# Long-short attention and a softplus FFN on one core: the same tasks issued in another sequence

## The chip, the cores and the metric

The program runs on one core of a Trainium2 chip. The core has five engines that work side by side, each through its own queue of instructions, strictly in order: TensorE (PE, matrix products; its weight loads appear apart as PEld), VectorE (DVE), ScalarE (ACT), GpSimd (POOL), and SyncE (SP), which here issues all transfers between device memory and on-chip memory. The metric is device time in microseconds for one execution.

## The reference

The inputs are q, k, v (4 batches, 8 heads, 768 positions, 64 wide) and two weight matrices. Every query looks at the keys less than 16 positions away and at 24 block summaries: of each block of 32 positions the elementwise maximum of the keys and the mean of the values. The result goes through a feed-forward network (FFN) with softplus between two products.

```python
k_sum = k.reshape(B, H, nb, block, D).max(axis=3)
v_sum = v.reshape(B, H, nb, block, D).mean(axis=3)
scores_l = scale * np.matmul(q, k.transpose(0, 1, 3, 2))
mask_l = np.abs(pos[:, None] - pos[None, :]) < window
scores_s = scale * np.einsum('bhsd,bhnd->bhsn', q, k_sum) + np.log(block)
scores_all = np.concatenate([np.where(mask_l, scores_l, -1e9), scores_s], axis=-1)
a = softmax(scores_all)
attn = np.matmul(a, np.concatenate([v, v_sum], axis=2))
h = x @ w_in            # x: 3072 tokens x 512, w_in: 512 x 2048
g = np.maximum(h, 0.0) + np.log1p(np.exp(-np.abs(h)))
return g @ w_out        # w_out: 2048 x 512
```

## The kernel before

**Tiling.** The 3072 tokens are six groups of 512. A group is two chunks of 256 queries, and each chunk is done for two head pairs at a time (hp 0 and 2). One such attention step is: scores on PE (line 653), mask and row maximum on DVE (666), exponent and row sum on ACT (674), inverse of the sum on DVE (681, 682), normalization on POOL, DVE or ACT (687, or eight instructions at 690), a transposition (for the first group on PE, for later ones on DVE at 720, and then out to device memory and back, 727 and 732), the product with the values on PE (751), and a copy of the result (763).

**The FFN.** The 2048 hidden columns are 16 blocks f. For float32 accuracy every operand is kept as a high part and a remainder, and a product takes three matmuls. The first product of groups 0 and 1 over blocks 0 to 7 is plain (line 1055); elsewhere a pair of blocks and two halves of the tokens are multiplied with seven products in place of eight (1095), which DVE combines from PSUM (the additions of line 1105, and a copy at 1114 or 1115). Softplus is two ACT instructions (1157, 1161) and a remainder on DVE (1165). The second product (1172) accumulates in PSUM.

**Operands.** Splitting a weight tile is a chain through one scratch tile t: magnitude (929 on DVE, 932 on ACT), clamp (936), shift (940), sign (944), tail (950 on ACT, 953 on DVE), addition of the tail on POOL (958), high part (962), remainder (969). Sums of weights for the seven-product form are joined (995), combined (1003 to 1006), rounded (1019) and given a remainder (1026) in a scratch tile ws. The sums of v of a batch are made in a scratch tile st (393 to 398), the maxima of k read a scratch tile kf. The attention's results are prepared in the same manner (differences at 821 and 822, high part at 806, remainder at 813). The tiles t, ws, st, kf and the output tile ob share one ring of two buffers, so a tile is only given out when the one two before it is done.

**The phases.** Blocks 0 to 7 for groups 0 to 4, then all 16 blocks for group 5, then blocks 8 to 15 for groups 4 down to 0. Attention of a group runs beside the FFN of the group before. The first half of the weights is split early in the kernel, the second half beside group 5's FFN. Below, f5.10 is block 10 of group 5.

**What sets the order.** All work is first recorded as 2346 numbered tasks with their reads, writes and buffers; a task may have several ways, each on another engine. Then a table written out in the source, SEQUENCE, gives the task numbers in the order in which they are issued; a letter behind a number picks another way than the first ("a" the second, "b" the third). Each engine gets its instructions in the order of this table. Waits come from the data and buffers alone.

```python
for word in sequence.split():
    task = self.tasks[int(word.rstrip("abc"))]
    assert all(other in begun for other, _ in task.after) and task not in begun
    begun.add(task)
    task.ways[" abc".index(word[-1]) if word[-1] in "abc" else 0].run()
```

Of the kernel before, what the change touches and what calls it, by code (L numbers as in the profile page):

```python
# [147 lines left out]
0 4 5 6 7 8 9 10 11 12 13 14 15 16 17 18 19 20 21 150 22 23 24 25 26 48 44 45 49 46 54 55 60 151 3 47 52 94 27 66 28  # L148
29 30 31 160 67 152a 50 156a 153 32 100 33 34 80 35 68 169 36 37 38 39 2 40 41 311 1 154 155 42 43 312 101 81 157 56
314 69 51 161a 53 106 61 162 165a 158 163 62 70 313 164 310 178 107 71 73 82 159 102 120 83 170 72 166 171 174 172 173  # L150
121 319 74 108 109 57 96 84 63 322 175 167 176a 58 177 168a 95 110 183a 64 103 65 323 122 370 123 59 187 97 179a 180
341 181 182 324 344 371 75 104 98 343 342 184 185 325 85 186a 340 99 105 374 326a 78 76 327 86 196 79 87 88 89 77 197
111 188a 189 113 90 92 134 349a 91 112 190 93 352 387 191 388 389 114 135 138 124 192 115 193 125 127 375 118 116 117
126 353 128 198 194 390 206 328 315 316 129 119 141 130 202 199 200 132 396a 354 391 201 244 133 215 195a 131 207 355
321 208 317 203 147 209 211 204 329 318 253 245 216 205 399 210 246 254 356 247 372 248 332 249 357 400 250 251 260
252 320 255 234 261 256 212 213 262 263 330 257 137 331 139a 214 144a 333 225 221 376 136 258 373 217 218 259 219 220
377a 264 334 358 417 418 265 345 346 401 419 267 421 222 266 268 223a 380 224 359 402 362 235 230 226 338a 145 420 227
228 361 146 148 274 229 350 403b 351 269 347 404 360 348 140 275 270 336a 381 378 271 231 276 277 405 278 232a 272 233
382 363 379 339a 392 393 236 364 366 368 369 142 237 238 335 281 288 367a 406 282 383 289 426 429 240 283 273 239 430
279 337a 280 290 409 408 407 384 291 531 149 532 284 285 385a 530 143 431 395 394 535a 386 292 295 432 296 538 397 286  # L160
398 297 433a 434 410 298 555 539 241 242 556 243 411 415a 416 435 513a 554 514 422 518 425 519 299 424 287 293 294 413
428 540 423 414 520a 559 303 436 541 437 439 562 302 515 438 300 301 542a 427 543 516 440 441 517a 579 563 578 445 581
582 580 443a 564 544 444 446 533 447 754 587 448 565 536 755 449 590 521a 450 537 758 566 545 451 304 608 611 534 456
457 305 458 567 609 546 548 452 453 610 459 463 464 607 759 465 307a 308a 466 454 547 460 549 591 550a 306 309 568
616a 467 522a 557 561 619 772 773 775 592 455 470 471 558 477 523a 524 756 560 593 478 774 525a 569 570 571 594a 595
461 572 462 472 620 771 473 596 552 766 551 474 757 479 780 573 783 480 762 583 585 481 621 484 485 574a 589 588 486
622 767 623 597 760 763 624 598 487 599 600 584 784 586 764 800 625 488 802 803 576a 468 469 475 476 601 801 785 799
602a 761 612 615 768 613 617 626 553 786 628 604 808a 491 492 493 605 614 765 811 627 498 499 577 618 787 482 788 606
629 603 828 789 575 494 500 812 1051 501 769 495 502 813 770 630 1053 829 631a 635 827 636 633 638 639a 640 641 365
483 642 776 814 634a 643a 777 778 637 644 489 647 645a 815b 832a 650 648 646 655 1052 649 651 653 652 1054 835 656 654  # L170
816 657 658 790 792 782 1055 781 836 659 490 496 412 660 497 503 666 667 853 854 793 837 526 505 852 661 668 527a 528a
857 504 1056 860 671 838 839a 507 672 817 506 529a 674 680 840 662 677 673 510 861 675 678 682 779 683 791 442 996 681
# [24 lines left out]
1351 1352a 1683a 1687a 1344a 1353a 1354 1355 1360 1363 1357 1358 1356 1361 1359 1365 1362 1367 1239 1366 1364 1690a
1369 1368 1370 1240 1376 1377 1371 1378 1237 1236 1372 1456 1241 1242 1457 1458 1459 1818 1461 1474 1243 1381 1460
1382 1387 1384 1385 1383 1386 1388 1392 1389 1390 1462 1391 1393 1394 1475 1476 1479 1463 1373 1374 1396 1375 1379
1395 1477 1397 1401 1478 1402 1398 1403 1406 1408 1814 1492 1464a 1811 1693a 1480 1481a 1482 1493 1407 1409 1412 1380  # L200
1410 1417 1415 1808 1411 1494 1413 1549 1550 1497 1495 1418 1416 1421 1419 1422 1496 1420 1551 1414 1426 1427 1399
1465 1400 1552a 1423 1428 1498 1499a 1404 1431 1500 1554a 1483 1434 1437 1432a 1435 1553a 1433 1438 1511 1488 1470
1405 1436 1439 1501 1442 1440 1512a 1513 1514 1516 1555 1441 1556 1502 1443 1446 1447 1515 1444 1424 1445 1425 1429
1430 1451 1557 1448 1466 1452 1517 1518 1453 1507 1467 1566 1569 1468 1469 1568 1471 1572 1519 1567a 1570 1472a 1484a
# [1159 lines left out]
```

## Time and profile before

| | |
|---|---|
| three runs | 690.67, 693.21, 697.65 us (median 693.21) |
| the profiled execution | 692.42 us |
| its span, first to last instruction | 690.7 us |
| mean granted TensorE clock | 0.973 |
| busy: PE, PEld, DVE, ACT, POOL | 619.7, 531.2, 489.2, 329.1, 243.2 us |
| moved by DMA | 103.41 MB, mean 150 GB/s |

A view of the trace groups instructions by line, engine, operation and tiles; "x<-r,x 128x512" means that tile x was written from tiles r and x. In groups, the number behind the comma is the mean of one in ns, and what follows the second bar is the idle time before these instructions and who ended it. In a timeline the columns are the start and the duration in us. In the list of waits, "A <- B: total, times, longest" says that A waited for B. The granted clock is the share of full speed that PE was given.

### The profile page before, as it was taken

The numbers are of one execution on the slowest core, as the hardware profiler recorded it, in microseconds if no ns is written. First come the engines' busy times: TensorE is split into PE (matmuls) and PEld (weight loads), VectorE is DVE, ScalarE is ACT, GpSimd is POOL, SyncE is SP. The second block draws the span as 40 slices with busy tenths as digits, with TensorE's granted clock in tenths as the row PEclk, the third lists the DMA queues.
The fourth block names the chain that finished last, engine by engine and source line by source line (L and its number), as shares of the span: only waits on it lengthen the run. The fifth ranks groups of instructions, "written<-read, shape, count | busy, mean of one in ns | idle before, by whom it ended". The sixth has DMA issues, their size and how long they took to land.

```text
span 690.7 us, 13155 instructions
## 1 busy us (share of the span) xinstructions
PE 619.7 (90%) x4880; PEld 531.2 (77%) x4880; DVE 489.2 (71%) x1143; ACT 329.1 (48%) x807; POOL 243.2 (35%) x204
## 2 busy tenths in 40 slices
PE   8876877979989889989989786988999999999997
PEld 8655665767778769878868665777989889899896
DVE  5999878776986676577768898986555655654542
ACT  4785755586686553946615364562331422313220
POOL 4465455425524150131145745463050600502000
PEclk9998999899999999999999998999999999999999
DMA  9888886689997966478345431001313112030031
GB/s 291 184 272 228 244 226 192 196 265 263 240 295 212 228 180 202 149 199 246 125 151 199 151 124 62 0 16 47 123 61 123 33 60 93 1 121 1 21 103 61
DMA packets 86848, 103.41 MB, mean 150 GB/s; under 512 B 27424, under 2 KB 64896, under 8 KB 86016
## 3 DMA queue, kind: packets, MB, share of 16 engines
q1 hardware_dynamic: 86784, 102.58, 50.1%
q8 instruction: 38, 0.62, 0.4%
q14 instruction: 26, 0.21, 0.1%
HBM read 72.88 MB, written 27.26 MB: 145 GB/s over the span
## 4 chain that ended last, share of the span: by engine, by line
PE 54%; DVE 20%; DMA 8%; ACT 6%; SPq 5%; POOL 4%; issue 4%; DVEq 0%; POOLq 0%; ACTq 0%
PE po L1172 24%; PE hx L1095 14%; PE hy L1095 10%; PE xo L751 3%; DMA st<-v_hp_dram 2%; PE sc L653 2%; DVE t L936 2%; DVE sp L666 2%; DMA pT<-squares 1%; DVE w L969 1%; DVE x L813 1%; SPq L732 1%; ACT sp L674 1%; DVE gl L1165 1%; DVE t L944 1%
## 5 line engine op out<-in xcount | busy, mean ns | idle before, releaser
L1172 PE MATMUL po<-w,gh 128*128 128x512 f32 x768 | 207.0, 398 | 0.5 <-ACT gh L1157 0.5
L1172 PEld LDWEIGHTS po<-w,gh 128*128 128x128 f32 x768 | 142.4, 191 | 31.1 <-issue 1.1
L1172 PE MATMUL po<-w,gl 128*128 128x512 f32 x384 | 117.6, 400 | 3.5 <-DVE gl L1165 2.2
L813 POOL TENSOR_TENSOR x<-r,x 128x512 fp32r<-128x512 f32 x36 | 48.3, 1354 | 183.7 <-ACT x L806 100.1
L1157 ACT ACTIVATE gh<-hx 128x512 fp32r<-128x512 f32 x40 | 24.0, 599 | 141.7 <-DVE hx L1105 141.6
L1095 PE MATMUL hx<-x,w 128*128 128x256 f32 x480 | 72.7, 288 | 15.5 <-DVE gl L1165 8.3
L1172 PEld LDWEIGHTS po<-w,gl 128*128 128x128 f32 x384 | 70.7, 190 | 19.8 <-DVE gl L1165 4.6
L1095 PE MATMUL hx<-x,sw 128*128 128x256 f32 x480 | 74.8, 292 | 9.8 <-DVE u L1105 8.0
L1095 PEld LDWEIGHTS hx<-x,w 128*128 128x128 f32 x480 | 65.8, 192 | 22.2 <-DVE gl L1165 10.5
L1095 PEld LDWEIGHTS hx<-x,sw 128*128 128x128 f32 x480 | 64.5, 193 | 13.7 <-DVE u L1105 9.4
L674 ACT ACTIVATE sp<-sp,nm 128x120 f32<-128x120 f32 x192 | 73.0, 382 | 4.1 <-DVE nm L666 3.8
L1095 PE MATMUL hy<-x,sw 128*128 128x256 f32 x480 | 67.9, 285 | 0.7 <-DVE x L813 0.7
L1095 PEld LDWEIGHTS hy<-x,sw 128*128 128x128 f32 x480 | 62.4, 192 | 1.1 <-DVE x L813 0.9
L958 POOL TENSOR_TENSOR t<-t,raw 128x1024 int32<-128x1024 int32 (+1 forms) x20 | 40.3, 2014 | 58.1 <-DVE t L944 33.2
L1055 PE MATMUL ph<-xw,w 128*128 128x512 f32 x192 | 50.2, 410 | 5.1 <-DVE xw L785 4.5
L1055 PEld LDWEIGHTS ph<-xw,w 128*128 128x128 f32 x192 | 36.3, 194 | 15.3 <-DVE xw L785 5.0
L666 DVE CUSTOM_DVE_ANT_0 sp<-sc,added 128x120 f32<-128x120 f32 x192 | 40.7, 277 | 3.4 <-PE sc L653 1.8
L687 POOL TENSOR_TENSOR sp<-sp,ss 128x960 f32<-128x960 f32 x14 | 25.9, 1849 | 48.1 <-ACT x L806 15.5
L1105 DVE TENSOR_TENSOR u<-hy,u 128x256 f32<-128x256 f32 x80 | 30.9, 420 | 14.3 <-PE hy L1095 13.7
L1165 DVE TENSOR_TENSOR gl<-hy,gh 128x512 fp32r<-128x512 f32 x40 | 27.5, 687 | 18.0 <-ACT hy L1161 17.8
L751 PEld LDWEIGHTS xo<-pT,v 120*64 120x64 f32 x640 | 21.0, 140 | 23.6 <-issue 14.9
L751 PE MATMUL xo<-pT,v 120*64 120x64 f32 x640 | 23.6, 227 | 16.3 <-DMA raw<-r 5.3
(115 smaller groups left out, 1036.8 us busy)
## 6 DMA issues: line engine op xcount, KB each, us to landing
squares<-tb SPq DMA_DIRECT2D x20, 512.0 KB
pT<-squares SPq DMA_DIRECT2D x80, 128.0 KB
raw<-w_out_dram SPq DMA_DIRECT2D x16, 512.0 KB
kf<-kT_dram SPq DMA_DIRECT2D x16, 384.0 KB
raw<-w_in_dram SPq DMA_DIRECT2D x6, 1024.0 KB
q<-qT_dram SPq DMA_DIRECT2D x20, 256.0 KB
raw<-r SPq DMA_DIRECT2D x20, 256.0 KB
part<-ob SPq DMA_DIRECT2D x10, 512.0 KB
```

The source lines that it names most:

```text
L666: nc.vector.tensor_tensor_reduce(out=sp()[:, n], in0=unit(n), in1=added()[:, kinds.index((lows[w], lows[w + 1]))], scale=-SCALE, scalar=FL ...
L674: nc.scalar.activation(sp()[:, n], sp()[:, n], AF.Exp, bias=nm()[:, n:n + 1], scale=-1.0, accum_out=ss()[:, n:n + 1],)
L687: engine.tensor_tensor(sp(), sp(), s, op=ALU.mult)
L751: nc.tensor.matmul(xo()[h * D:(h + 1) * D, g * CH + w * QW:g * CH + (w + 1) * QW], lhsT=tiles.v(g)[:, w, h * D:(h + 1) * D], rhs=queries(g ...
L813: engine.tensor_tensor(to(1), a(), to(0).bitcast(F32), op=ALU.subtract)
L958: nc.gpsimd.tensor_tensor(a, a, word(0, I32), op=ALU.add)
L1055: nc.tensor.matmul(ph(), lhsT=lhs(part, cc), rhs=xw[cc][0]()[:, xw[cc][1], a], start=cc == 0 and n == 0, stop=cc == NCC - 1 and n == 2,)
L1095: nc.tensor.matmul(to()[:, half], lhsT=lhs(wa, cc), rhs=of_x(xa)[:, cc * CH:(cc + 1) * CH], start=cc == 0 and m == 0, stop=cc == NG - 1 an ...
L1105: DVE, dve(CH), lambda: nc.vector.tensor_tensor(out(), a(), b(), op=op), reads, [write],
L1157: nc.scalar.activation(gh(), all_of(), AF.Softplus)
L1165: nc.vector.tensor_sub(out=gl(), in0=all_of(), in1=gh().bitcast(F32))
L1172: nc.tensor.matmul(po[t](), lhsT=a()[:, t * P:(t + 1) * P], rhs=w2()[:, part, i2 * DM:(i2 + 1) * DM], start=f == f0 and i == 0, stop=f == ...
```

## The change

Only the table SEQUENCE differs. The tasks, buffers, transfers and their sizes are the same; 151 tasks run on another engine. In all, ACT has 27 tasks more, POOL 16 fewer, DVE 11 fewer. The numbers stay close to their old places (the last quarter is nearly unchanged). Its first lines, and one from the late weight stage:

```diff
-0 4 5 6 7 8 9 10 11 12 13 14 15 16 17 18 19 20 21 150 22 23 24 25 26 48 44 45 49 46 54 55 60 151 3 47 52 94 27 66 28
+160 161a 162 163 0 4 44 46 54 3 5 6 7 8 9 10 11 12 13 14 15 164 165 45 60 151 2 166 47 1 167a 152a 168 55 169 16 17 18
...
-1465 1400 1552a 1423 1428 1498 1499a 1404 1431 1500 1554a 1483 1434 1437 1432a 1435 1553a 1433 1438 1511 1488 1470
+1438 1512a 1405 1436 1516 1555 1439 1442 1443 1513 1446 1444 1556 1424 1425 1445 1514 1515 1451 1447 1429 1452 1517
```

By engine, tasks that move: high parts of attention results from DVE to ACT (17, and 5 back) and their remainders between POOL and DVE (14 to POOL, 12 to DVE), remainders of weights (8) and of weight sums (4) from POOL to DVE, magnitudes (6) and high parts (6, 4 back) of weights from DVE to ACT, normalizations (5 from POOL to DVE, 3 from POOL to ACT), the first copy of a block pair (7 each way between ACT and DVE). The transfers stay on SP, with loads of q, k, v and weights at other places in its queue; the first of all is now a weight tile.

DVE before, late weight stage, from f5.8's two remainders (gl) over the weight sum ws of blocks 12 and 13 to f5.10's first combinations (u):

```order
L1165 TENSOR_TENSOR gl<-hx,gh 128x512
L1165 TENSOR_TENSOR gl<-hy,gh 128x512
L995 TENSOR_TENSOR ws<-w 128x2x2x128 x2
L1003 TENSOR_TENSOR ws<-ws 128x256
L1004 TENSOR_TENSOR ws<-ws 128x256
L1005 TENSOR_TENSOR ws<-ws 128x256
L1006 TENSOR_TENSOR ws<-ws 128x256
L1105 TENSOR_TENSOR u_4914<-hx,p_4900 128x256
L1105 TENSOR_TENSOR u_4922<-hy,u_4914 128x256
```

The same place on DVE now:

```order
L1165 TENSOR_TENSOR gl<-hx,gh 128x512
L1165 TENSOR_TENSOR gl<-hy,gh 128x512
L944 SCALAR_TENSOR_TENSOR t<-raw,t 128x1024
L969 TENSOR_TENSOR w<-t,w 128x512
L995 TENSOR_TENSOR ws<-w 128x2x2x128 x2
L1105 TENSOR_TENSOR u_4930<-hx,p_4905 128x256
L1105 TENSOR_TENSOR u_4932<-hy,u_4930 128x256
```

The four combining instructions of ws have gone to POOL, a remainder of a weight tile (L969) has come from POOL, and a sign (L944) that stood ahead of the gl now stands behind them.

DVE before, some 35 us earlier, from the last combinations of f5.4 to the joined weight sum and f5.6's copy (p):

```order
L1105 TENSOR_TENSOR hy<-u_4578,hy 128x256
L1105 TENSOR_TENSOR hy<-hy,u_4578 128x256
L1019 CAST sw<-ws 128x1024
L1165 TENSOR_TENSOR gl<-hx,gh 128x512
L1165 TENSOR_TENSOR gl<-hy,gh 128x512
L962 CAST w<-t 128x1024
L969 TENSOR_TENSOR w<-t,w 128x1024
L995 TENSOR_TENSOR ws<-w 128x2x2x128 x2
L1115 COPY p_4668<-hx 128x256
```

And now:

```order
L1105 TENSOR_TENSOR hy<-hy,u_4605 128x256
L1105 TENSOR_TENSOR hy<-u_4605,hy 128x256
L1165 TENSOR_TENSOR gl<-hx,gh 128x512
L1165 TENSOR_TENSOR gl<-hy,gh 128x512
L1026 TENSOR_TENSOR sw<-ws,sw 128x1024
L969 TENSOR_TENSOR w<-t,w 128x1024
L995 TENSOR_TENSOR ws<-w 128x2x2x128 x2
```

The rounding of the weight sum (L1019), the high part of a weight tile (L962) and the copy p are on ACT now; the weight sum's remainder (L1026) has come from POOL.

ACT now, at group 1's first blocks, with the third group's attention (sp, scores) between them:

```order
L674 ACTIVATE sp,ss<-sp,nm 128x120 x8
L1157 ACT_TABLE_LOAD
L1157 ACTIVATE gh<-ph 128x512
L1161 ACTIVATE ph<-ph 128x512
L690 ACTIVATE sp<-sp,ss 128x120 x8
L1157 ACTIVATE gh<-ph 128x512
L1206 COPY ob<-po 128x512 x2
L1157 ACTIVATE gh<-ph 128x512
L1161 ACTIVATE ph<-ph 128x512 x2
```

The normalization L690 (eight instructions) was on POOL; it stands between the softplus of one block and that of the next.

More of the change, by code (lines that the diff above doesn't have):

```diff
@@ L153 @@
[L153 to L172, printed above, removed]
@@ new lines @@
+405 382 363 240 285 236 337a 338 420 237 364 366 288 368 238 383 142 406 426 369a 239 289 429 407 430 290 241 409 392
+291 143 140 384 385a 295 386 296 367 531 532 279 530 280 393 535 538 242a 395 394 431 145a 365 432 433b 408 397 243
+292 297 286 513 398 555 298 410 434 556 146 559a 539 554 518a 435 299 422 425 411a 287 293 514 423 428 540 413 519a
+427 415 436 541 520 542a 439 562 294 543 437 515 563 303 516 301 517 302 300 438 416a 424 440 441 578 443 445 446 579
+444 582 521 339a 414a 580 581 544 533 587 564 447 456 448 590 534 565 754 457 536 755 545 449 450 758 546 547 548 608
@@ new lines @@
+451 307a 609 610 611 759 566b 458 537 463 308a 607 464 304 305 567 465 309 459 466 452 453 616a 454 306 591 460 592
+619 467 568 756 772 549 550 455 522a 774 775 557 523a 593 594a 524 560 569 470 471 570 571 472 148 552a 477 478 461
+462 473 595 474 561 620 479 572 558 525a 480 573 481 757 553a 773 551 771 780 596 766 484 485 621 760 783 574 622 468
+623a 469 583 584 589 486 597 475 761 767 588 598 487 585 599 800 600 586 803 576 624 784 476 601 762 802 785 577 801
+488 625 764 763 612 799 786 602a 604 605a 768 787b 626 788 627 491 492 628 808 493 618 629 613 615 498 494 765 769
@@ new lines @@
+665 669 864a 688 691 1007 1024 692 1062 693 865 1008 794 795 1025 1027 818 670 819 696 699 1009 698 1026 804 702 1032a
+805 821 820 697a 700 707 703 701 705 709 706 689 690 708 694 1010 806 704 710 711 810 1023 716 712 807 809 1059 866
+1063 717 713 718 822 823 1035 721 727 722 796 842 830 724 1011 797a 1012 1069 825 834 831 1036 723 844 725 726 728
+1068 845 843 729 732 730 833 734 731 733 736 735 737 741 1070 695 798 714 742 738 743 846 824 1072 847a 1071 715 719
+720 1037 826a 1077 1080 739 849a 1013 850 851a 1060 1064 867 868 1038 855 859 870 856 858 869 1039b 1040 1081 871 740
@@ new lines @@
+848 872 874 1098 1097 876 879 1099 1065 877 882 880 878 881 1100 744 883a 884a 1066 875 885 891 886 894 888 889 887
+1041 895 896 890 745 892 898 897 748a 1101 1082 749a 899 893 1083 1000 1106a 1084 900 901 907 902 1001 908 1006 1014
+1002 1015 1109 1017 1016 909 1003 1005 1085 747 746 903 1018 1110 1245 1246 1019 873 1021 904 912 1067 915 914 918 913
+1249 1244 916 750 751a 921 919 917 923 752a 924 922 925 1042 920 926 927 905 928 1086 929 932 933 906 910 1111 934
+1020 937 1028 1034 1029 1031 940 938a 943 941 948 944 946 949 939 947 942 952 953 911 950 1033 945 951 957 958 954
@@ new lines @@
+1022a 930 1112 1252 1045 1030 753 1044 1043 1113 1268 959 1046 1114 1047 931 1269 962 1253 963 1087 964 965 968 1073
+1088 1272a 966 971 967 973 1267 1090 1078 969 975 972 976 1074 1075 974 1049 935 936 1115 1050 1275 1079 977 978 1076
+970 982 983 1089 1291 1048 979 984 1091 1092a 1094 1116 1254 1095 1299a 1117 1255 1256 1102 955 956 1118 1103 1105
+1104 1257 1119 1108 960 961 980 1107 1120 1276 1096a 1121a 1093 1125 1290 1123 1258 1292 1293 1294 1126 1259 1128 1131
+1127 1261 1129 1130 981 1124 1132a 1133a 1134 1140 985 1135 1143 1137 1247 1251 1277 1260 1144 1136 1138 1145 1139
@@ new lines @@
+1557 1448 1466a 1453 1566 1572 1467 1468 1469 1569 1567a 1570 1518 1568 1501 1571 1471 1430 1811 1573 1577 1519 1472
+1473 1484a 1575 1578 1576 1502 1485 1486 1503a 1579 1581 1574 1504 1530 1580 1487 1489 1505 1582 1583 1586 1587 1588
+1490 1506 1449 1450 1454 1591 1592 1593 1491 1507 1558a 1597 1594 1595 1596 1598 1455 1600 1520 1508 1599 1535 1602
+1509 1601 1603 1559 1604 1606 1605 1607 1611 1612 1510 1608 1584 1613 1560a 1585 1531a 1521 1589 1561 1532 1616 1618
+1617 1625 1533 1619 1534 1522a 1523 1622 1590 1626 1536 1620 1539 1540 1545 1537 1621 1623 1624 1627 1628 1524 1629
@@ new lines @@
+1631 1609 1610 1630 1525 1538 1636 1614 1632 1637 1562a 1526 1615 1527 1563a 1564 1633 1638 1641 1565 1642 1650 1644
+1528 1647 1643 1529 1645 1691 1648 1646 1652 1651 1692a 1634 1653 1687a 1541a 1685 1635 1649 1654 1542 1543 1639 1656
+1544 1655 1657 1694 1640 1658 1661 1662 1663 1546 1686 1695 1688 1809 1689 1812 1942 1948 1696 1699 1702 1697a 1698
+1700 1701 1703 1705 1707 1547 1706 1709 1708 1548a 1659 1711 1704 1710 1810 1660 1712 1718 1713 1719 1815 1720 1664
+1723 1726 1725 1724a 1729 1727 1952 1728 1730 1665 1668a 1734 1732 1733 1736 1735 1669 1666 1738 1813a 1667 1671 1714
```

109 lines of the change are left out of this document (47 added, 62 removed), and 4 rows, old and new, of the table SEQUENCE.

## The prediction

> **What bounds the kernel now.** I read the page's busy shares first, then a table of stages, then the waits inside the two stages that stand out, then single instructions.
>
> ```profile
> PE 619.7 (90%) x4880; PEld 531.2 (77%) x4880; DVE 489.2 (71%) x1143; ACT 329.1 (48%) x807; POOL 243.2 (35%) x204
> 0.00:47.00 47.00, 39.28 (x641) 33.87 (x641) 37.41 (x131) 29.79 (x109) 23.36 (x42) 0.96 0.90 255
> 47.00:127.00 80.00, 61.72 (x451) 46.89 (x450) 69.39 (x152) 45.58 (x115) 46.50 (x37) 0.89 0.78 217
> 127.00:181.00 54.00, 47.94 (x415) 37.60 (x415) 39.32 (x113) 38.26 (x110) 22.14 (x20) 0.97 0.89 257
> 181.00:247.00 66.00, 58.26 (x574) 49.95 (x573) 49.05 (x159) 42.11 (x122) 23.15 (x21) 1.00 0.85 234
> 247.00:355.00 108.00, 103.74 (x952) 88.99 (x951) 75.77 (x210) 61.14 (x170) 22.53 (x16) 1.00 0.60 179
> 355.00:405.00 50.00, 41.23 (x251) 35.16 (x250) 45.01 (x69) 23.97 (x37) 28.50 (x23) 1.00 0.50 175
> 405.00:462.00 57.00, 46.68 (x261) 40.92 (x260) 50.78 (x74) 30.94 (x41) 28.98 (x15) 0.91 0.10 37
> 462.00:477.00 15.00, 10.92 (x63) 10.00 (x62) 12.27 (x16) 3.75 (x6) 9.19 (x6) 0.89 0.16 52
> 477.00:691.00 214.00, 209.96 (x1288) 187.79 (x1286) 110.22 (x224) 53.58 (x101) 38.87 (x29) 1.00 0.20 65
> ```
>
> A stage row gives its length, then busy time of PE, weight load, DVE, ACT and POOL, the granted clock, the DMA share and GB/s. From 247 to 355 and from 477 on, PE is busy for 314 of 322 us at full clock: nothing that only reorders the other engines can help there. PE idles 18 us in 47 to 127 and 23 us (8.8, 10.3, 4.1) in 355 to 477. In both DVE is the busy one (87%, and 108 of 122 us), POOL is at its heaviest (58% and 55%) and the clock is below one. These are the stages in which weights are split into parts. Between them, 127 to 247, DMA is at 85 to 89% and PE loses 14 us. Who ends PE's waits in 350 to 480:
>
> ```profile
> PE hx L1095 <- DVE u L1105: 12.4, 6, 4.3
> PE hx L1095 <- DVE gl L1165: 8.3, 5, 2.9
> ```
>
> So 20.7 us of the late idle time are waits for two kinds of cheap DVE instructions that come late because others stand ahead of them. The longest wait is this one (DVE, then POOL, then PE):
>
> ```profile
> 418.89 0.68 DVE L1165 TENSOR_TENSOR gl<-hy,gh 128x512 fp32r<-128x512 f32 x1
> 419.49 2.53 DVE L995 TENSOR_TENSOR ws<-w 128x512 f32<-128x512 f32 x2
> 422.06 2.60 DVE L1003 TENSOR_TENSOR ws<-ws 128x256 f32<-128x256 f32 x1
> 424.69 0.43 DVE L1004 TENSOR_TENSOR ws<-ws 128x256 f32<-128x256 f32 x1
> 425.95 0.42 DVE L1105 TENSOR_TENSOR u<-hx,p 128x256 f32<-128x256 f32 x1
> 422.03 2.34 POOL L969 TENSOR_TENSOR w<-t,w 128x1024 fp32r<-128x1024 f32 x1 [1.16 <-ACT w L962]
> 420.55 0.89 PE L1095 MATMUL hx<-x,sw 128*128 128x256 f32 x6
> 426.42 1.44 PE L1095 MATMUL hx<-x,sw 128*128 128x256 f32 x5 [4.26 <-DVE u L1105]
> ```
>
> L1003 and L1004 are the same size, yet one took 2.60 us and the other 0.43: the long one ends just after POOL's L969 (422.03 + 2.34 = 424.37). POOL makes DVE slow. The Trainium skill, page "SBUF — State Buffer", section "SBUF: two separate sides", says why: DVE and GpSimd share one port pair as an exclusive lock, held for a whole instruction by a GpSimd instruction or by a DVE one with two SBUF inputs or in a two-port mode. These rows agree.
>
> **The change, part by part.** All tasks, buffers and transfers stay; the sum of PE's work stays. Sums are made against the profiled execution, 692.42 us (span 690.7 and 1.7 around it), 0.8 us under the median of 693.21.
>
> ```profile
> 126.73 1.66 PE L1055 MATMUL ph<-xw,w 128*128 128x512 f32 x6
> 133.34 0.69 DVE L1165 TENSOR_TENSOR gl<-ph,gh 128x512 fp32r<-128x512 f32 x1 [1.14 <-ACT ph L1161]
> ```
>
> *Part A, start to the second group's first products.* Up to that group's first remainder, the second row here, I compared what the two sequences put on each engine, each at the shortest record of its form. POOL loses 8 tasks and 20.3 us (67.0 to 46.7): three normalizations, two sums of v, two remainders of weight sums and others. DVE has 5 tasks fewer but 2.9 us more (104.6 to 107.5). ACT gets 11 more, 13.0 us. Forms on the two engines:
>
> ```profile
> L969 POOL TENSOR_TENSOR w<-t,w 128x1024 fp32r<-128x1024 f32 x5 | 13.3, 2662 | 9.3 <-ACT w L962 6.7 <-DVE w L962 2.6
> L969 DVE TENSOR_TENSOR w<-t,w 128x1024 fp32r<-128x1024 f32 x7 | 9.1, 1298 | 0.1
> L687 POOL TENSOR_TENSOR sp<-sp,ss 128x960 f32<-128x960 f32 x14 | 25.9, 1849 | 48.1 <-ACT x L806 15.5 <-DVE ss L682 13.1 <-ACT hx L1161 10.1
> 174.51 2.44 POOL L393 TENSOR_TENSOR st<-st 96x512 f32<-96x512 f32 x2 [0.62 <-DMA st<-v_hp_dram]
> 103.60 1.15 DVE L393 TENSOR_TENSOR st<-st 96x512 f32<-96x512 f32 x2 [0.91 <-DMA st<-v_hp_dram]
> L936 DVE TENSOR_SCALAR t<-t 128x1024 f32<-128x1024 f32 x12 | 14.3, 1190 | 1.0 <-ACT t L932 0.9
> 459.03 0.69 DVE L940 TENSOR_SCALAR t<-t 128x1024 uint32<-128x1024 uint32 x1
> ```
>
> The same subtraction (L969) takes half as long on DVE as on POOL. What POOL costs DVE is seen in L936: it averages 1190 ns, where a like instruction that nobody hinders takes 690 (last row). Added up in this way over all DVE records to 134 us, 24.1 us of DVE's time there are hindrance, 0.36 us for each us of POOL's 67.0. With 20.3 us of POOL gone DVE gets back 7.3, less the 2.9 it takes on: 4.4 us. The scratch tiles (two buffers, t, st, kf, ws share them) are given back sooner as well, because the two large adds of a sum of v (L393) hold its tile for 1.15 us on DVE and for 2.44 on POOL. Not all of it lasts: behind this stage the transfers are at 89%. I carry 2.5 us on; the ends are 7 gained, if the shorter tile times count too, and 3 lost, if the 2.9 us of DVE work stand in front of what PE waits for and POOL's absence gives nothing back.
>
> *Part B, 134 to 363 us.* DVE gives up 6.8 us of 174 (2 of them five combinations that merely fall into part C's count), POOL takes 4.0 more, ACT 7.7 more. DVE is no bound there (39.3 of 54, 49.0 of 66, 75.8 of 108 us). Loads of k and v change places by a few issues in SP's queue, the transposed tiles' four reads stand one to three issues earlier. An issue is about half a microsecond, and many are hidden:
>
> ```profile
> 134.61 0.47 SPq L732
> ```
>
> I take 0, with 3 gained to 5 lost.
>
> *Part C, the late weight stage.* Counted in the same way from 363 to 469 us: POOL 50.6 to 34.2 us (ten tasks fewer), DVE 73.7 to 82.1 (eight more, five of them the combinations just named, so 6.4 us in truth), ACT 45.0 to 50.4. Ten remainders leave POOL's stretch, nine of them for DVE. At this stage's rate of hindrance (26.8 us on 50.6 of POOL, 0.53) DVE gets back 8.7 and takes on 6.4: 2.3 in sum. But PE waits for places, not for sums, and two places change:
>
> ```profile
> 385.61 2.86 DVE L1019 CAST sw<-ws 128x1024 fp32r<-128x1024 f32 x1 [1.46 <-POOL ws L1006]
> 388.39 0.68 DVE L1165 TENSOR_TENSOR gl<-hx,gh 128x512 fp32r<-128x512 f32 x1
> ```
>
> L1019 goes to ACT and the remainder L1165 behind it no longer waits. PE's wait at 389 (the 2.9 in the second wait row) loses its cause: minus 2.9. At 426 the four instructions L1003 to L1006 go to POOL and behind the combinations; 425.95 less 422.06 is 3.9 us that no longer stand ahead of L1105, and a remainder of 0.7 that is new there does: minus 3.2. Against that, three remainders and a rounding that DVE takes over come before PE's waits at 450 and 469: plus 1 (0.7 to 4, by whether POOL's absence pays for them). So C is minus 5, nearer to the places than to the sum; its ends are minus 11, with the wait at 469 gone too (4 us), and plus 3.
>
> By the skill's rule the lock is what counts: POOL's 16.4 us less and about 6.4 us more on DVE are 10 us less of locked time, so C would be minus 10 and the whole 680.
>
> *Part D, ACT's tables.* The order has 40 table loads instead of 38, both more before 127 us, where ACT is busy 45.6 of 80 us: hidden by its idle time, 2.6 us if not.
>
> ```profile
> 161.59 1.28 ACT L1157 ACT_TABLE_LOAD   x1 [5.46 <-PE ph L1055]
> ```
>
> Sum: 692.4 - 2.5 + 0 - 5 + 0 = 684.9, rounded to **685 us**. What is late next at the two places is PE's own queue at 389, and at 426 the join L995, still ahead of L1105.
>
> **The rivals.** *ACT becomes the bound (slower).* Place: the third and fourth attention chunks, 127 to 181 us. There the change puts two normalizations on ACT, eight instructions each, and some roundings. Behind them in ACT's queue stands the softplus that PE waits for.
>
> ```profile
> L690 ACT ACTIVATE sp<-sp,ss 128x120 f32<-128x120 f32 x32 | 9.6, 383 | 6.6 <-DVE ss L682 6.6
> POOL sp L687 <- DVE ss L682: 6.5, 2, 3.7
> ACT gh L1157 <- PE ph L1055: 8.0, 4, 3.2
> ACT L1157 <- PE ph L1055: 5.5, 1, 5.5
> ```
>
> The last three rows are waits in that stage. Two normalizations are 16 times 383 ns, 6.1 us, and they wait for DVE's inverse as POOL's did (6.5 us): up to 12.6 us in which ACT does nothing else. Against it: ACT itself waited for PE for 13.5 us there, which is the point from which it decides; with some 2 us of roundings more it is just passed. If all 12.6 land on PE and C brings 4: 692.4 + 12.6 - 4 = 701.
>
> *Given back.* DVE's sum is what counts, not the places: A melts into the transfers, C is the computed minus 2.3, part D takes 1 of its 2.6: 691. For it speaks DVE's 89% in 355 to 477; against it that 20.7 us are waits for named instructions.
>
> *Much more.* The waits shrink so far that the half-clock stretches go. In 47 to 127 the clock is 0.89 and in 405 to 477 0.91 and 0.89: 8.8, 5.1 and 1.7 us of clock lost, 15.6; at 426 it shows as 1.44 us for five matmuls against 0.89 for six. If half goes on top of 8.5 for A and C: 692.4 - 8.5 - 7.8 = 676. The Trainium skill ("TensorE: Matmul & The Clock Gate", section "What's actually happening") puts the half clock down to an idle window of about 3.4 us; the wait of 4.26 at 426 fits, so one below 3.4 us should not cost it.
>
> **How the numbers follow.** The forecast has 0.55, its own range 679 to 691, and about two thirds of it lie over 1% under the median (below 686.3; 1% is about what a measurement of this kernel can tell). Given back 0.15, much more 0.10, ACT 0.20 (three quarters of it above 700.1). Faster: 0.35 + 0.10 = 0.45. Slower: 0.15. Within 1%: 0.20 + 0.15 + 0.05 = 0.40. The range, 672 to 701, leaves out the far half of the slower case and the tail of the faster ones.
>
> **What would show it.** Right, if the new table of stages has POOL some 15 us lower before 127 us and again in the late stage, L936's mean falls well below 1.19 us, the DVE records of L1003 fall to 0.43, and PE's waits for L1105 and L1165 late in the kernel fall from 20.7 to some 14. A is wrong if the first hidden product of the second group does not start earlier than 126.7 us. C is wrong if the stage from f5's first combination to 477 is as long as before. The forecast is wrong as a whole if ACT's softplus is named as the releaser of PE's waits in 127 to 181.

## The result, and the profile after

The changed kernel takes 664.8 us (median of 4 runs, 663.3 to 668.3) beside 691.9 us for the kernel before on the same chip: 0.960 of it, 95% interval 0.953 to 0.967. A second set of runs gave 664.9 us and 0.955 (0.952 to 0.959). The prediction was 685, its range 672 to 701: the direction is right, the gain was 27 us instead of 8.

First the busy line of the page after, then the table of stages. Its cuts are the same events as before (first product of f0.0, f1.0, f2.0, f3.0, f5.0, f5.8, f4.8, f4.10), at their new times. Columns: length, busy time of PE, weight load, DVE, ACT and POOL, granted clock, DMA share, GB/s.

```profile
PE 615.8 (93%) x4880; PEld 528.1 (80%) x4880; DVE 447.1 (68%) x1132; ACT 356.1 (54%) x857; POOL 206.5 (31%) x188
0.00:54.50 54.50, 40.94 (x641) 35.84 (x641) 35.05 (x135) 35.53 (x116) 26.65 (x43) 0.87 0.84 240
54.50:117.30 62.80, 57.12 (x451) 43.98 (x449) 53.34 (x134) 52.99 (x133) 26.76 (x22) 0.97 0.89 249
117.30:172.20 54.90, 48.77 (x422) 37.73 (x421) 41.52 (x130) 44.44 (x131) 17.51 (x19) 1.00 0.99 259
172.20:233.70 61.50, 58.61 (x573) 49.73 (x572) 44.67 (x153) 42.16 (x120) 24.76 (x24) 1.00 0.89 253
233.70:339.80 106.10, 102.88 (x948) 89.03 (x947) 70.16 (x204) 61.06 (x165) 26.16 (x20) 1.00 0.61 183
339.80:382.50 42.70, 39.56 (x243) 34.01 (x242) 37.93 (x71) 25.85 (x39) 19.63 (x17) 1.00 0.54 184
382.50:439.00 56.50, 49.11 (x270) 42.53 (x269) 48.82 (x74) 34.90 (x46) 19.46 (x13) 0.91 0.15 53
439.00:447.60 8.60, 8.60 (x58) 7.84 (x57) 7.48 (x15) 3.79 (x7) 4.52 (x4) 1.00 0.27 91
447.60:661.60 214.00, 210.25 (x1288) 187.45 (x1286) 108.12 (x223) 55.33 (x104) 41.03 (x31) 1.00 0.19 65
```

Where the 29.1 us between the two spans (690.7 and 661.6) come from: the start is 7.5 us longer (54.5 against 47.0), the stage f0.0 to f1.0 is 17.0 shorter (62.8 against 79.8), f1 is 0.9 longer, f2 5.3 shorter, f3 and f4 1.8, f5.0 to f4.10 13.4 shorter (107.8 against 121.2); the last stretch has its 214 us as before. So part A gave 9.5, part B 6.2, part C 13.4. In the stage f0.0 to f1.0 PE's busy time fell by 4.3 us, while the clock rose from 0.89 to 0.97, and its waits fell from 18.2 to 5.7 us. The four longest before:

```profile
PE ph L1055 <- DVE xw L785: 4.5, 1, 4.5
PE sc L653 <- DVE ss L681: 3.2, 1, 3.2
PE xo L751 <- DMA raw<-w_in_dram: 2.9, 1, 2.9
PE po L1172 <- DVE gl L1165: 2.2, 1, 2.2
```

Of the 18.2 us, 11.5 hung on DVE and 6.2 on transfers; after the change these are 1.5 and 1.9.

DVE is busy 42 us less, though its tasks, each at the shortest record of its kind, add up to 3 us more (453 against 450; the records of neighbouring instructions overlap a little, so sums of records lie above the busy time). What went is lengthening. Two single instructions, by form, mean in ns behind the busy time; the first row is of before, the other two are of after:

```profile
L1003 DVE TENSOR_TENSOR ws<-ws 128x256 f32<-128x256 f32 x4 | 3.9, 965 | 0.1
L936 DVE TENSOR_SCALAR t<-t 128x1024 f32<-128x1024 f32 x12 | 10.7, 891 | 6.1 <-ACT t L932 6.0
L1003 DVE TENSOR_TENSOR ws<-ws 128x256 f32<-128x256 f32 x3 | 1.3, 419 | 0.1
```

L936 fell from 1190 to 891 ns, L1003 from 965 to 419 (its fourth task is on POOL now). PE's waits from 339.8 to 447.6, where 20.7 us hung on u and gl before:

```profile
PE hx L1095 <- DVE u L1105: 4.3, 4, 2.2
PE hx L1095 <- DVE gl L1165: 3.2, 1, 3.2
```

### The profile page after: what moved, and what is told of

It reads as the page before. It is cut to its first block, busy times and chain, and to the rows that moved or that the text cites. A ratio compares the mean times of both kernels' runs of the same rounds, so it can differ in the third digit from the quotient of the medians.

```text
span 661.6 us, 13174 instructions
## 1 busy us (share of the span) xinstructions
PE 615.8 (93%) x4880; PEld 528.1 (80%) x4880; DVE 447.1 (68%) x1132; ACT 356.1 (54%) x857; POOL 206.5 (31%) x188
## 3 DMA queue, kind: packets, MB, share of 16 engines
q1 hardware_dynamic: 86784, 102.58, 52.4%
## 4 chain that ended last, share of the span: by engine, by line
PE 56%; DVE 15%; DMA 8%; ACT 7%; issue 7%; SPq 4%; POOL 2%; DVEq 0%; ACTq 0%; POOLq 0%
PE po L1172 25%; PE hx L1095 14%; PE hy L1095 10%; PE xo L751 2%; DMA raw<-w_out_dram 2%; PE sc L653 2%; DVE sp L666 2%; DVE u L1105 2%; DMA squares<-tb 1%; SPq L732 1%; ACT sp L674 1%; DMA v<-v_hp_dram 1%; PE warm L1257 1%; DVE ws L995 1%; DVE hx L1105 1%
## 5 line engine op out<-in xcount | busy, mean ns | idle before, releaser
L1095 PE MATMUL hx<-x,sw 128*128 128x256 f32 x480 | 73.3, 288 | 4.7 <-DVE u L1105 3.8
L1095 PEld LDWEIGHTS hx<-x,w 128*128 128x128 f32 x480 | 65.9, 191 | 12.8 <-DVE gl L1165 4.2
L958 POOL TENSOR_TENSOR t<-t,raw 128x1024 int32<-128x1024 int32 (+1 forms) x20 | 42.8, 2140 | 89.2 <-DVE t L944 25.8
L1095 PEld LDWEIGHTS hy<-x,sw 128*128 128x128 f32 x480 | 62.8, 192 | 0.3
L1055 PE MATMUL ph<-xw,w 128*128 128x512 f32 x192 | 48.0, 400 | 3.1 <-DVE gl L1165 2.7
L666 DVE CUSTOM_DVE_ANT_0 sp<-sc,added 128x120 f32<-128x120 f32 x192 | 40.8, 277 | 8.0 <-PE sc L653 6.1
L1055 PEld LDWEIGHTS ph<-xw,w 128*128 128x128 f32 x192 | 35.4, 188 | 12.8 <-DVE gl L1165 3.4
L806 ACT CAST x<-r 128x512 fp32r<-128x512 f32 x45 | 27.2, 618 | 33.4 <-PE hx L1095 11.9
L1165 DVE TENSOR_TENSOR gl<-hx,gh 128x512 fp32r<-128x512 f32 x40 | 27.5, 687 | 19.3 <-ACT hx L1161 19.2
L1105 DVE TENSOR_TENSOR u<-hy,u 128x256 f32<-128x256 f32 x80 | 30.8, 419 | 12.4 <-PE hy L1095 11.3
L1095 PE MATMUL hy<-x,w 128*128 128x256 f32 x240 | 37.0, 290 | 2.3 <-DVE u L1105 1.4
L1165 DVE TENSOR_TENSOR gl<-hy,gh 128x512 fp32r<-128x512 f32 x40 | 27.5, 687 | 13.5 <-ACT hy L1161 13.5
```

The source lines that it names most:

```text
L666: nc.vector.tensor_tensor_reduce(out=sp()[:, n], in0=unit(n), in1=added()[:, kinds.index((lows[w], lows[w + 1]))], scale=-SCALE, scalar=FL ...
L806: copy(out=to(0), in_=a())
L958: nc.gpsimd.tensor_tensor(a, a, word(0, I32), op=ALU.add)
L1055: nc.tensor.matmul(ph(), lhsT=lhs(part, cc), rhs=xw[cc][0]()[:, xw[cc][1], a], start=cc == 0 and n == 0, stop=cc == NCC - 1 and n == 2,)
L1095: nc.tensor.matmul(to()[:, half], lhsT=lhs(wa, cc), rhs=of_x(xa)[:, cc * CH:(cc + 1) * CH], start=cc == 0 and m == 0, stop=cc == NG - 1 an ...
L1105: DVE, dve(CH), lambda: nc.vector.tensor_tensor(out(), a(), b(), op=op), reads, [write],
```

## The experiments

In all of them the measure is the ratio to the kernel before on the same chip (changed kernel: 0.960 and 0.955), and the time of PE's first product of a block in the trace. For the two stages that DVE limits I split DVE's time over all its records: the length of each instruction at the shortest record of its kind in any of these traces (unhindered), what it took beyond that (lengthening), and the rest. A task that begins ahead of a cut counts whole. Neighbouring records overlap by some 0.05 to 0.1 us, so the rest is less than DVE's idle time: in the late stage it is 6.9 and 5.5 us, where DVE is idle for 13.5 us both before and after. In the diffs a line is the part of a longer line of the table in which the change stands.

**Engines alone, order alone.** Engines alone gives 151 words of the old table the new engine; order alone does the reverse.

```diff
-29 30 31 160 67 152a 50 156a 153 32 100 33 34
+29 30 31 160 67 152a 50 156 153 32 100 33 34
```

> The old order of tasks, with each task on the engine that the new table gives it. Theory 'amount' (POOL's share of the work slows DVE, whatever stands beside it; the changed kernel has 37 us less of POOL): most of the 27 us gained are here, 668 to 676 us, and DVE's busy time falls from 489 to about 455. Theory 'place' (what counts is which DVE instruction runs while POOL works, and that the order sets): little of it, 684 to 695 us, DVE stays above 470. Theory 'together' (neither half works without the other): no faster than before, 690 or more.

> The new order of tasks, with each task on its old engine. Theory 'amount': little gained, 686 to 692 us, DVE's busy time stays near 485. Theory 'place': much of the gain, 672 to 680 us, with DVE's busy time below 465 although POOL's work is the old one. Theory 'together': 690 or more.

Measured: engines alone 715.2 us, 1.030 (1.024 to 1.036); order alone 712.7 us, 1.024 (1.017 to 1.031). Either half alone makes the kernel slower. Only the "together" theory expected that. Busy lines of the two pages, engines alone first:

```profile
PE 633.1 (89%) x4880; PEld 538.6 (76%) x4880; DVE 461.0 (65%) x1132; ACT 357.7 (50%) x859; POOL 204.3 (29%) x188
```

```profile
PE 626.2 (88%) x4880; PEld 533.3 (75%) x4880; DVE 466.5 (66%) x1143; ACT 330.5 (47%) x807; POOL 243.8 (34%) x204
```

In both, DVE is busy far less than the 489.2 us of before, and both are slower: a lower sum on DVE gained nothing here by itself. PE's longest waits in the stage f0.0 to f1.0 and in f5.0 to f4.10 with engines alone (total, times, longest):

```profile
PE po L1172 <- DVE gl L1165: 7.3, 3, 4.8
PE ph L1055 <- DVE xw L785: 4.2, 1, 4.2
PE hx L1095 <- DVE gl L1165: 12.7, 4, 7.8
```

and in order alone, f0.0 to f1.0:

```profile
PE po L1172 <- DVE gl L1165: 9.2, 2, 6.5
PE xo L751 <- DMA v<-v_hp_dram: 5.4, 1, 5.4
```

**Early part alone, late part alone.** The new table up to f1.0 and then the old one; the old one up to f5.0 and then the new one (tasks already issued left out).

> The new table up to the second group's first hidden products (f1.0), then the old one. In the changed kernel these products start 9.5 us earlier (117.3 against 126.7). If that is kept to the end: 682 us. If it melts into the transfers behind it, as the prediction had it: 688 to 690 us.

> The old table up to f5.0's first product, then the new one. In the changed kernel the stretch from there to the first product of f4.10 takes 107.8 us against 121.2. If this is the late stage's own: 678 to 680 us. If it needs the earlier parts (tiles or weights prepared ahead): over 685. The prediction's minus 5 would give 687.

Measured: 685.7 us, 0.987 (0.982 to 0.993), and 679.1 us, 0.977 (0.973 to 0.982). In the first, f1.0 starts 8.2 us earlier than before, and 6.7 us of that are left at the end: most of what is gained early is kept and does not melt in the transfers behind it. In the second the stretch from f5.0 to f4.10 gains 14.4 us by itself. With part B's 6.2, which no run changes alone, the parts add up to 27 of the 29 us.

**Which engine's moves.** The new order, with the 74 moves to or from POOL undone, or the 77 between DVE and ACT.

```diff
-152a 168 55
+152a 168a 55
```

> The new order, with the 74 tasks that the change moves to or from POOL back on their old engines; the 77 moves between DVE and ACT stay. If POOL's work is the cause of the gain: 695 to 715 us, as with all old engines (712.7). If any mismatch of order and engines costs alike: 685 to 700 us. If POOL's moves count for little: 665 to 675.

> The new order, with the 77 tasks that the change moves between DVE and ACT back on their old engines; the 74 moves to and from POOL stay. If POOL's work is the cause of the gain: 665 to 675 us. If any mismatch of order and engines costs alike: 685 to 700 us.

Measured: 699.5 us, 1.005 (1.003 to 1.008), and 690.5 us, 0.992 (0.989 to 0.995). Neither kind carries the gain alone; undone, they cost some 31 to 35 and 22 to 26 us. The split of DVE's time, in us, with POOL's work at its shortest records behind it:

| stage | kernel | length | unhindered | lengthening | rest | POOL |
|---|---|---|---|---|---|---|
| start to f1.0 | before | 126.7 | 97.9 | 26.4 | 2.5 | 64.5 |
| | changed | 117.3 | 96.5 | 7.5 | 13.3 | 46.9 |
| | engines alone | 134.2 | 100.4 | 19.1 | 14.6 | 46.9 |
| | order alone | 136.8 | 97.1 | 13.5 | 26.2 | 60.7 |
| | POOL undone | 131.7 | 92.2 | 11.5 | 28.0 | 60.7 |
| | ACT undone | 132.9 | 104.0 | 15.3 | 13.6 | 46.9 |
| f5.0 to f4.10 | before | 121.2 | 82.3 | 31.9 | 6.9 | 59.9 |
| | changed | 107.8 | 87.5 | 14.7 | 5.5 | 40.8 |
| | engines alone | 124.9 | 87.9 | 17.9 | 19.1 | 42.0 |
| | order alone | 113.2 | 81.3 | 24.8 | 7.1 | 58.6 |
| | POOL undone | 111.1 | 77.8 | 17.1 | 16.1 | 58.6 |
| | ACT undone | 110.7 | 91.0 | 16.3 | 3.4 | 40.8 |

Engines alone has the changed kernel's 46.9 us of POOL in the first stage, and 19.1 us of lengthening where that has 7.5. So the lengthening does not follow POOL's amount. With POOL's moves undone the rest is 14.7 and 10.6 us longer than in the changed kernel. In the late stage part of this hangs on POOL by name (DVE waits 3.5 us for its remainders L969). In the first stage the longest wait named is for ACT's magnitudes (L932, 20.6 us instead of 14.0), so that POOL's late results are behind it is not shown there. With ACT's undone DVE has 3.5 to 7.5 us more to do.

**What POOL costs DVE, by itself.**

```python
for beside, engine in ((none, G), (add_1024, G), (subtract_512, G), (scalar_engine, S)):
    beside()       # POOL's or ACT's instructions, one after the other
    dve_forms()    # eight of each form
```

> A kernel of its own that leaves out the whole computation: DVE runs seven forms of this kernel's instructions, eight of each, four times over: alone, beside POOL's 128x1024 additions (L958's form), beside POOL's 128x512 subtractions (L969's form), beside ACT's copies. Theory 'amount' (each us of POOL costs DVE the same, whatever DVE does): all forms are lengthened alike, by 30 to 50%. Theory 'place' (it depends on what DVE does): forms that work in SBUF alone with one input (L936's and L962's, 0.69 us alone) or two (L821's, 0.68) come out at 1.2 us or more, forms with an input in PSUM (L1165's 0.69, L1105's 0.43) within 0.1 us of their length alone. Beside ACT: no change in either.

Measured, DVE's groups (count, busy us, mean ns) alone:

```profile
L72 DVE SCALAR_TENSOR_TENSOR dl<-a,b 128x1024 uint32<-128x1024 uint32 x8 | 9.8, 1224 | 0.2
L68 DVE CAST wr<-a 128x1024 fp32r<-128x1024 f32 x8 | 5.5, 693 | 0.2
L70 DVE TENSOR_TENSOR lr<-a,b 128x512 fp32r<-128x512 f32 x8 | 5.5, 691 | 0.2
L76 DVE TENSOR_TENSOR gr<-h,a 128x512 fp32r<-128x512 f32 x8 | 5.5, 690 | 0.2
```

beside POOL's 128x1024 additions (h is in PSUM, the memory that PE writes its products to; all else is in SBUF, the other on-chip memory):

```profile
L70 DVE TENSOR_TENSOR lr<-a,b 128x512 fp32r<-128x512 f32 x8 | 21.8, 2725 | 0.2
L68 DVE CAST wr<-a 128x1024 fp32r<-128x1024 f32 x8 | 21.8, 2725 | 0.2
```

and beside its 128x512 subtractions:

```profile
L72 DVE SCALAR_TENSOR_TENSOR dl<-a,b 128x1024 uint32<-128x1024 uint32 x8 | 17.4, 2180 | 0.2
L70 DVE TENSOR_TENSOR lr<-a,b 128x512 fp32r<-128x512 f32 x8 | 13.2, 1647 | 0.2
L76 DVE TENSOR_TENSOR gr<-h,a 128x512 fp32r<-128x512 f32 x8 | 5.5, 690 | 0.2
L78 DVE TENSOR_TENSOR du<-h,a 128x256 f32<-128x256 f32 x8 | 3.4, 423 | 0.2
```

A form that works in SBUF alone goes from 0.69 to 2.73 us beside the one and to 1.65 beside the other: it waits for nearly one whole POOL instruction each time. A form with an operand in PSUM keeps its 0.69 or 0.42 us to the hundredth; beside ACT nothing changes. POOL's 28 additions were over at 129.7 us, before DVE came to the forms with PSUM at 134.4, so this kernel tests those forms beside the subtractions only. For the additions the changed kernel has the rows, a remainder that starts within an addition and keeps its 0.68 us:

```profile
436.85 2.45 POOL L958 TENSOR_TENSOR t<-t,raw 128x1024 int32<-128x1024 int32 x1 [3.89 <-issue]
436.97 0.68 DVE L1165 TENSOR_TENSOR gl<-hx,gh 128x512 fp32r<-128x512 f32 x1
```

Over the traces of all runs of the whole kernel, no record of L1105 or L1165 beside POOL, more than 2300 of them, is more than 0.06 us above the shortest. The "place" theory stands. It does not hold for every form in SBUF: the transposition L720 (1.23 to 1.25 us) and the reduction L365 (0.90 to 0.96 us) stay as short beside POOL. The Trainium skill, page "SBUF — State Buffer", section "SBUF: two separate sides", says that the shared port pair is locked for a whole instruction, by a GpSimd instruction or by a DVE instruction with two SBUF inputs or in a two-port mode; these rows agree.

Counted over the traces, this is the change in the late stage (f5.0 to f4.10): POOL is busy 65.8 us before and 43.6 after; beside it DVE runs SBUF-only forms for 37.1 us before and 14.7 after, and forms with PSUM for 21.9 and 22.0. All of what left POOL was time beside the forms that suffer. Engines alone has 18.1 there, order alone 30.3. A record that waits for POOL counts here with its wait, so this is the lengthening seen from POOL's side and no second proof of it.

**POOL's work put back.** 16 subtractions that nobody waits for, in POOL's queue of the changed kernel, without any other edit: once where DVE limits, once where PE does.

```diff
+            if word == "d":
+                self.dose()
+                continue
...
+    dosed = const.tile([P, 480], F32, name="dosed")
+    nc.gpsimd.memset(dosed, 0.0)
+    order.dose = lambda: nc.gpsimd.tensor_tensor(dosed, dosed, dosed, op=ALU.subtract)
```

> The changed kernel with 16 idle subtractions more on POOL (128x480, on a tile of their own that nobody reads, some 1.2 us each, 19 us in all), spread over the table from f5.0 to f4.10. No task, engine or order is changed. If DVE's lengthening costs time: at the changed kernel's own rate there (14.5 us on 40.8 us of POOL, 0.36) 7 us on DVE, and the kernel 4 to 9 us longer (669 to 674). If only the places in the queues count: within 1.5 us of 664.9, with the lengthening in the trace.

> The same 16 subtractions, spread from f3.8 to f1.8, where PE is busy all the time and DVE has more than half of its time idle. Both theories: within 1.5 us of 664.9. A longer time would mean that the subtractions cost something other than DVE's time.

Measured: 673.8 us, 0.970 (0.966 to 0.974), in the late stage, and 665.1 us, 0.958 (0.954 to 0.962), at the end. The group, and PE's waits from f5.0 to f4.10 (line numbers are six higher than elsewhere):

```profile
L309 POOL TENSOR_TENSOR dosed<-dosed 128x480 f32<-128x480 f32 x16 | 17.9, 1120 | 0.2
PE hx L1101 <- DVE u L1111: 5.6, 6, 2.9
PE hx L1101 <- DVE gl L1171: 5.3, 3, 4.1
PE hy L1101 <- DVE x L819: 2.9, 1, 2.9
```

The same 17.9 us of idle work cost 9 us in one place and nothing in the other; the stretch f5.0 to f4.10 is 115.8 us beside 107.8 and 104.8 in two traces of the changed kernel. In its trace DVE's lengthening there is 22.7 us instead of 14.7, while its unhindered work (87.5) and the rest (5.6) are as in the changed kernel: the 8.0 us more of the stretch are lengthening, and not a wait for POOL's own results, which the idle work also delays. So in this stage the lengthening itself costs the time, half a microsecond for each of POOL's.

**The prediction's two places.**

```diff
-1470 1422 1420 1423 1400 1426 1427 1404 1552 1428
+1470 1422 1420 1552a 1423 1400 1426 1427 1404 1428
...
-1449 1450 1454 1591 1592 1593 1491 1507 1558a 1597
+1449 1450 1454 1591 1592 1593 1491 1507 1558a 1559a 1597
```

> The new table with the prediction's two late places undone: the rounding L1019 of f5.6's weight sum goes back to DVE ahead of the two remainders L1165, and the four combining instructions L1003 to L1006 of the sum for blocks 12 and 13 go back to DVE ahead of f5.10's combinations. By the prediction's prices (2.9 and 3.2): plus 6, 671 us. If these prices were mostly POOL's hindrance, which is less in the changed kernel: the clean lengths, 0.7 and 4 times 0.42 us, plus 2.4 at most, 665 to 667 us.

Measured: 668.4 us, 0.961 (0.959 to 0.964). From f5.4 to f5.6 it is 0.8 us longer than in the two traces of the changed kernel and from f5.6 to f5.8 0.5, from f5.8 to f5.10 as long, from f5.10 to f5.12 1.8 to 3.3 longer, of which f5.12 to f5.14 gives 0.3 to 1.6 back. The first place is worth about its clean length, not 2.9; the second lies between its clean length (1.7) and about the predicted 3.2. The whole time can't be told from the changed kernel's first ratio, 0.960.

**The late start.** The old table up to f0.0 and then the new one (run twice), the changed kernel again beside it, and the new table with one wait of the start removed.

```diff
-64 74 179a 97 110a 122 180 181 182 370 65 59 98
+64 74 179a 101 102 97 103 110a 122 180 181 182 370 65 59 98 104
```

> The old table up to the first product of f0.0, then the new one. In the changed kernel this product starts 7.5 us later (54.5 against 47.0), with 9.7 us of idle time on DVE ahead of it. If the late start is a plain loss of the new table: 655 to 660 us. If it is an advance (weights of the next tiles prepared there, 2.7 us more on DVE and 5.5 on ACT) that the stage behind it draws on: 664 to 670.

> The changed kernel once more, as a measure for the two beside it: 0.955 to 0.965 of before.

> The kernel of e5 again. If its 662.6 was a real gain over the changed kernel: 2 us faster than e10. If the earlier f0.0 is paid back by f1.0, as its trace has it (6.2 us ahead of before there, where the changed kernel is 9.5 ahead): within 1.5 us of e10.

> The new table, in which the third and fourth heads' v of the first chunk is loaded, summed and averaged as early as in the old table (PE waited 7.3 us for the averages at 48.1). If the late start of f0.0 comes from that wait: f0.0 starts at about 50 and the kernel takes 660 to 663 us. If DVE's and ACT's work on the weights sets it: f0.0 or f1.0 as late as in the changed kernel, within 1.5 us of e10.

Measured: the old start 662.6 us, 0.953 (0.949 to 0.956), and again 663.0, 0.953 (0.948 to 0.957); the changed kernel 664.9, 0.955 (0.952 to 0.959); the start unblocked 662.9, 0.953 (0.949 to 0.957). These can't be told apart: the 2 us by which the old start is ahead lie within the intervals. In the traces the old start has f0.0 2.8 us earlier than the changed kernel and f1.0 3.2 later, so what it saves is paid back by f1.0. That the late start is an advance on the weights fits this, but no run shows it. With the wait removed f0.0 comes at 52.6, but the changed kernel's second trace has 52.4 too, so whether that wait matters stays open.

**The waits that are left.** e12 with three of DVE's late steps put behind what PE waits for; then the same with the copy ahead of the rounding on ACT.

```diff
-1632 1637 1562a 1526 1615 1527 1563a 1564 1633 1638
+1632 1637 1633 1638 1562a 1526 1615 1527 1563a 1564
...
-1633 1638 1562a 1526 1615 1527 1563a 1564 1641 1565 1642
+1633 1638 1562a 1615 1563a 1641 1642 1564 1526 1527 1565
```

> e12's start, and in the late stage three of DVE's steps put behind what PE waits for: the joined sum (L995) of blocks 12 and 13 behind f5.10's first three combinations, that of blocks 14 and 15 behind f5.12's two remainders (L1165), a clamp (L936) behind f5.12's combinations. PE's waits there in the changed kernel are 2.2, 3.2 and 1.1 us. If these waits are the places' own: 3 to 6 us less than e12, 657 to 660. If what is put off comes too late elsewhere: 661 or more.

> e15, in which f5.14's copy p (L1114) stands ahead of the rounding L1019 on ACT, and the tail L950 of the next weight tile behind it, so that POOL's L958 starts after the joined sum L995 is done. If lengthening and place are the cause: L995 takes 1.3 us instead of 3.5 for two, PE's wait for the copy (5.1 us) is gone, some 2 us remain for the rounded sum, and the late stretch is 2 to 3 us shorter than e15's 104.7. If the wait only moves again: 104 to 106 us.

Measured: 659.4 us, 0.951 (0.947 to 0.955), and 660.7 us, 0.951 (0.948 to 0.954). These are the two fastest, but their intervals overlap a little with that of the changed kernel's second set. In the late stretch (e12 104.7 us) the first is 104.4 and the second 104.2: the wait moves. In the first it comes back as

```profile
421.60 1.04 ACT L1019 CAST sw<-ws 128x1024 fp32r<-128x1024 f32 x1 [5.07 <-DVE ws L1006]
422.55 0.36 ACT L1114 COPY p<-hx 128x256 f32<-128x256 f32 x1
422.96 1.65 PE L1095 MATMUL hx<-x,w 128*128 128x256 f32 x6 [5.09 <-ACT p L1114]
```

and in the second, where the joined sum took 1.28 us instead of 3.49 since POOL no longer ran beside it, as

```profile
417.62 1.28 DVE L995 TENSOR_TENSOR ws<-w 128x512 f32<-128x512 f32 x2
428.13 1.65 PE L1095 MATMUL hx<-x,sw 128*128 128x256 f32 x6 [2.84 <-DVE u L1105]
```

DVE's lengthening there fell from 12.8 (e12) to 11.4 and 8.7 us, and the rest rose from 4.4 to 5.5 and 8.0. Of e16's first expectation the single steps came (L995, the wait for the copy, 1.9 us of PE's waits for the rounded sum), but not the shorter stretch; by its length the second held. The stage is no longer limited by POOL's lengthening alone.

## Why the prediction was right or wrong

**Bounds.** Right: DVE in the two weight stages, lengthened by POOL. Most of the time came from there. For the late stage e13 shows that lengthening costs time; for the first stage it is argued from the split and from PE's waits.

**Part A, minus 2.5: measured minus 9.5.** The term that failed is the rate: 0.36 us of lengthening per us of POOL was taken as fixed, so that 20.3 us less of POOL were worth 7.3. By f1.0 POOL had 17.6 us less and the lengthening fell by 18.9, from 26.4 to 7.5. The rate itself fell from 0.41 to 0.16; that the new order has POOL beside fewer of DVE's forms that wait is counted for the late stage only, and the reason for it here is argued. The 2.9 us more for DVE are there, but behind f1.0's first product (two remainders L1026 and a mask step L666 stand there, which the prediction's later cut takes in); up to it DVE has 1.4 less. Wrong too was that the gain melts to 2.5: e3 kept 6.7 of 8.2. Not foreseen were the start, 7.5 us longer, in which DVE idles 19.4 us instead of 9.6, and the 4.3 us less of waits for transfers between f0.0 and f1.0.

**Part B, 0: measured minus 6.2**, beyond its end of minus 3. The step that failed is that loads at other places are hidden and so worth nothing. PE's waits for transfers from 126.7 to 247.5, before:

```profile
PE xo L751 <- DMA pT<-squares: 3.9, 2, 2.4
PE xo L751 <- DMA raw<-r: 3.3, 1, 3.3
PE sc L653 <- DMA q<-qT_dram: 2.8, 2, 1.8
PE xo L751 <- DMA v<-vs: 1.9, 1, 1.9
```

and from 117.3 to 233.7, after:

```profile
PE xo L751 <- DMA raw<-r: 2.3, 2, 1.5
PE sc L653 <- DMA q<-qT_dram: 1.2, 2, 1.0
PE xo L751 <- DMA k<-kT_dram: 1.0, 2, 0.6
```

11.9 us became 4.5, while PE's waits for DVE there rose from 1.9 to 4.5. The sum had no term for these rows. That the loads' new places removed the first is argued from the rows; no run moved the loads alone. Of the 1.8 us less for f3 and f4, PE's waits hold about 1; what made the others is open.

**Part C, minus 5: measured minus 13.4.** The direct estimate by sum had DVE get back 8.7 and take on 6.4. It took on 5.2 (82.3 to 87.5), and got back 17.2 (31.9 to 14.7): again the fixed rate, here 0.53, was the failure, and 0.36 was found. The Trainium skill's rule taken as 10 us less of locked time was nearer, though it counted POOL's whole time and not what stands beside SBUF-only forms. The two places were read rightly, and L1003's records did fall to 0.42; but the first price, 2.9, was mostly lengthening that was gone anyway: undone, it cost 0.8, and the second, 3.2, cost 1.8 to 3.3. The end of minus 11 is more than its terms give (2.9, 3.2 and 4 make 10.1).

**Part D, 0.** Nothing seen of it; not tested apart.

**The rivals.** ACT as the bound did not come: from 117.3 to 172.2 no wait of PE names the softplus, and the stage took 0.9 us more. ACT's wait for DVE's inverse was there, and no wait of PE names it:

```profile
ACT sp L690 <- DVE ss L682: 3.9, 1, 3.9
```

"Given back" fell with e3. "Much more" was nearest, at 676: its clock part came early (0.89 to 0.97 in f0) and hardly late (0.91 remains from 382.5, only the 1.7 us of 462 to 477 are gained), and the start (0.96 to 0.87) lost 5.2 us of clock of the 6.9 that f0 gained.

**The signs named.** POOL was 16.5 us lower up to f1.0 (69.9 to 53.4), L936 fell, PE's waits for u and gl fell to 7.5, not to 14, f1.0 came at 117.3 instead of 126.7, and the late stage is shorter. The mechanism was right; the step that failed is the fixed rate of lengthening in parts A and C, and the zero for transfers in part B. No rival let the rate itself fall, which is why the range missed.

## What to carry to other kernels

Cost POOL by what runs beside it, not by its length: here a DVE instruction on SBUF tiles alone (the casts, the operations with a scalar, those on two tiles) waited for nearly a whole POOL instruction, and one with a PSUM operand for nothing, so sort the bottleneck's instructions by form and operands before pricing a move. Order and engine assignment of such queues are one thing: each half of this change alone cost some 17 to 21 us, both together gained 27. In a stage that one engine limits, split its time into unhindered, lengthening and rest, and look for what changes each.

## What the runs showed of the hardware that was not expected

With both engines issuing back to back, the lengthening is regular: DVE's record is its own length plus POOL's shortest less 0.30 us, within 0.02 us. Beside the additions (2.33 us at the shortest) 0.69 becomes 2.73; beside the subtractions (1.26) 0.69 becomes 1.65 and 1.22 becomes 2.18. POOL waits too: its median addition takes 2.67 us and its median subtraction 1.59. POOL's records, shortest, median and longest:

```profile
L91 POOL TENSOR_TENSOR pc<-pa,pb x52: 1258/1588/2123, 148.0 to 230.8; 128x512 f32<-128x512 f32 x52
L87 POOL TENSOR_TENSOR pc<-pa,pb x28: 2334/2668/3202, 51.1 to 126.5; 128x1024 int32<-128x1024 int32 x28
```

The half clock comes after shorter waits than the prediction allowed for. It said that a wait below 3.4 us should not cost it. In the changed kernel's late stage the granted clock is 0.50 from 401.2 to 404.5 and from 425.1 to 431.8 us, and the waits ahead of these are 2.20 and 3.21 us. Six matmuls that take 0.98 us at full clock take 1.46 there:

```profile
399.63 0.98 PE L1095 MATMUL hx<-x,w 128*128 128x256 f32 x6 [2.20 <-DVE u L1105]
401.15 1.46 PE L1095 MATMUL hy<-x,w 128*128 128x256 f32 x6
424.79 1.46 PE L1095 MATMUL hx<-x,w 128*128 128x256 f32 x6 [3.21 <-DVE gl L1165]
```

After the shorter wait the first six still ran at full clock, so the half clock set in 1.5 us behind it. The trace of the kernel before already had such a case: a wait of 2.05 us ahead of 450.0, and 0.50 from 452.3 to 455.6. The Trainium skill, page "TensorE: Matmul & The Clock Gate", section "What's actually happening", gives an idle window of about 3.4 us for it; these waits are 0.2 to 1.4 us below and disagree, by the idle time that the trace records.
